# VectorE's exponential sets: the second integer addition as an accumulating transfer issued by GpSimd

## The chip, the cores and the metric
The kernel runs on one core of one Trainium2 chip. The metric is the device time of one execution in microseconds (us); lower is better. Before the change two runs took 795.1 and 797.66 us, median 796.38 us. The profile comes from a further execution of the same program, which took 790.26 us.

## The reference
The output is `g * a + (1 - g) * b`, with x of 2048 rows by 512 columns in bf16:

```python
g = sigmoid((x * gate_w).sum(-1, keepdims=True))
# a: attention with 32 heads of 16 columns
scores = einsum("bhqd,bhkd->bhqk", q, k) * 16 ** -0.5
p = softmax(scores, axis=-1)
a = einsum("bhqk,bhkd->bhqd", p, v) ... @ wo
# b: a state-space convolution, 512 channels, 128 states
P = exp(logdA[:, :, None] * l)
K = einsum("dn,dnl,dn->dl", Cc, P, dB).real
b = causal convolution of x with K (written with FFTs) + x * Dskip
```

The attention needs 32 x 2048 x 2048 exponentials. They are the largest single piece of work outside TensorE.

## The kernel before
**Tiles, quads and blocks.** A score tile holds 128 keys by 512 queries of one head. There are 2048 of them (`NSL`). Four tiles of the same 128 keys and the same 512 queries, for four heads that TensorE handles side by side, form a quad. Sixteen quads, one for each of the 16 key tiles of the sequence, form a block; 32 blocks make up the attention. All value products of a block accumulate in one bank of PSUM, `OA`. When the last quad of a block has been added, VectorE transposes `OA` out (`norm_a`), and only then can the first quad of the next block be added.

**Groups.** The scores are computed three tiles at a time. Such a group fills one of two PSUM buffers, `SC0` and `SC1`, and there are 683 groups. `qk` (line 930) issues a group's score products on TensorE. `ex` (line 945) has ScalarE take the exponential of all three tiles, or of two of them where VectorE takes the third, and writes bf16 into `ET`, a ring of 15 tiles. `pv` (line 976) multiplies a quad from `ET` with the values `VE` into `OA`.

**Sets on VectorE.** Between groups 206 and 678 VectorE takes a share of the exponentials. A set is one quad: four consecutive groups each give one tile to VectorE and two to ScalarE (`SHAPE`, line 73). `bits` (line 981) computes an affine function of the scores and stores it as 16-bit integers in the set's buffer `DZ`; read as bf16 these bits are a rough exponential. To make it less rough, three versions are added up in the value product. `batch` (line 991) issues, in this order:

1. VectorE writes `DU = DZ + 42` (line 1003, through the helper at line 996).
2. TensorE multiplies `DZ` with `VE` into `OA` (line 1008).
3. TensorE multiplies `DU` with scaled values `VS` into `OA` (line 1011).
4. VectorE adds 84 to `DZ` in place (line 1013, line 996 again).
5. TensorE multiplies the new `DZ` with the other scaled values into `OA` (line 1015), and the set is marked `dvp{i}`.

Steps 2 and 3 wait until the set's block has begun (`pv{16b}`), and from the second set on until the set before is complete (`dvp{i-1}`, line 1006).

**Which quads become sets.** `WIN` (line 78) gives two stretches of groups. From 206 to 400 only key tiles 1, 5, 9 and 13 of a block may become sets, from 400 to 678 also 3, 7 and 11 (`VKT`). Each stretch has three pairs of buffers `DZ` and `DU`, taken in turn; `clear` (line 790) refuses a new set while the set that last used its buffer is not complete. `keytile` (line 801) takes the quad from the current block while more than `LEFT` = 3 quads of it are left, and otherwise from the next block. A set is started only where the planned VectorE idle time allows (`decide`, line 831, 0.3 us of idle for each set). The last quad of a block waits in `pvq` (line 879) for the last set of the block, since it closes the accumulation.

**The order of the work.** All five instruction streams are written out ahead of time by a planner (`Sched`, lines 315 to 447). It keeps a planned clock for each engine and, group by group, issues the segments of many threads (projections, tables, convolution, normalisation, sets) where they fit. What it decides is fixed in the program: each engine runs its own stream in order and waits on semaphores for the others. For a transfer, `dma` (line 248) plans a time `c` on the issuing queue and a latency `lat` after it, and `ready` (line 182) adds a margin `DMARG` of 1.2 us before a reader is placed.

**Other work in the same time.** The convolution loads its operands by DMA on the SP queue, `WT` in 128 transfers of 256 KB and `U` in 64 of about 286 KB, and TensorE multiplies them into the bank `MB`. TensorE also issues filler products with a zero tile `wm`. GpSimd's queue holds only a few memsets and iotas.

Of the kernel before, what the change touches and what calls it, by code (L numbers as in the profile page):

```python
# [11 lines left out]
ALU = mybir.AluOpType  # L12
# [57 lines left out]
STEP = ((42, 205 / 256), (84, 166 / 256))  # L70
XB = 128 * (127 - math.log2(3.15037))
VKT = ((1, 5, 9, 13), (3, 7, 11))
SHAPE = ((2, 1),) * 4
LEFT = 3
VSW = 152
VSP = [len(k) * VSW for k in VKT]
VSAT = (200, 390)
WIN = ((206, 400, 3, 1), (400, 678, 3, 2))
DVQ = (("tabs", 0.3), (None, 1e9))
BP = 2.2  # L80
DVCAP = 2.0
BUP = 1
# [375 lines left out]
def declare(nc, es):  # L458
    B = {}

    def sb(name, free, dt=BF16):
        B[name] = Buf(name, "sb", free, dt)
# [27 lines left out]

    sb("gwT", 4)
    sb("wm", D)
    sb("x0n", 4 * D)
    sb("idf", P, FP32)
    sb("idb", P)
# [143 lines left out]
def record(nc, p, B, ins):  # L639
# [165 lines left out]
    def quad():  # L805
        if not rem:
            plan["b"] += 1
            rem.extend(ahead or block(plan["b"]))
            ahead[:] = block(plan["b"] + 1)
        q = rem.pop(0)  # L810
        pend.extend(range(4 * q, 4 * q + 4))
        if not rem:
            ends[plan["b"]] = q
        if rem or q < NQ - 16:
            todo.append((q, plan["prev"], dvps.get(plan["b"])))
        plan["prev"] = q

    def take(n, ds):
# [12 lines left out]
    def decide(g):  # L831
        while len(tiles) < min(3 * g + 3, NSL):
            x = len(tiles) // 3
            plan["used"] = max(plan["used"], idle() - DVCAP)
            if plan["set"] is None and clear(x) and idle() - plan["used"] >= dvq():
                plan["used"] += dvq()
                of, c = keytile(x)
                of.remove(c)
                w = win(x)
                r = f"{w}{sum(st['w'] == w for st in sets) % WIN[w][2]}"  # L840
                old = [i for i, st in enumerate(sets) if st["r"] == r]
                plan["set"], plan["k"], dvps[c // 16] = len(sets), 0, f"dvp{len(sets)}"
                sets.append(dict(q=c, b=c // 16, w=w, r=r, z=B["DZ" + r], u=B["DU" + r], old=old[-1] if old else None, js=[]))
            if plan["set"] is None:
                tiles.extend(take(3, []))
            else:
                st = sets[plan["set"]]
                na, nd = SHAPE[plan["k"]]
                if not pend:
                    quad()  # L850
                nxt = [pend[i % len(pend)] % 4 for i in range(na)]
                ds = sorted((j for j in range(4) if j not in st["js"]), key=lambda j: j in nxt)[:nd]
                st["js"] += ds
                got = take(na, [4 * st["q"] + j for j in ds])
                tiles.extend(got + [4 * st["q"] + j for j in ds])
                if nd:
                    vec[x] = (plan["set"], len(st["js"]) - nd, nd)
                plan["k"] += 1
                if plan["k"] == len(SHAPE):
                    plan["set"] = None  # L860
            seat()
            while todo and all(4 * todo[0][0] + j in home for j in range(4)):
                sch.add(pvq(*todo.pop(0)), 0, LAG)
# [15 lines left out]
    def pvq(q, prev, wait):  # L879
        b, kt = divmod(q, 16)  # L880
        if prev is not None:
            yield ("AFTER", f"pv{prev}")
        if ends.get(b) == q and wait:
            yield ("AFTER", wait)
        if kt == 0 and b >= 1:
            yield ("AFTER", f"n{b - 1}")
        if b < 8 and b % 2 == 0:
            yield ("AFTER", f"V{b // 2}.{kt // 4}")
        yield ("PE", QUAD)
        pv(q)  # L890
        sch.mark(f"pv{q}")
        if ends.get(b) == q:
            sch.mark(f"end{b}")
            sch.open(None)
        else:
            sch.open(b)
# [68 lines left out]
    def vscaled(k):  # L965
        kts = VKT[k]
        yield ("AFTER", f"g{VSAT[k]}")
        for pi in range(4):
            for step, (_, f) in enumerate(STEP):
                yield ("DVE", .25)  # L970
                op("DVE", lambda v, pi=pi, step=step, f=f: v.tensor_scalar(VS[k]((4 * step + pi) * VSP[k], [[VSW, len(kts)], [1, VSW]]),
                                                                           VE(pi * 4 * VG + kts[0] * VW, [[VG, len(kts)], [1, VSW]]), f, None, ALU.mult),
                   [(VE, (pi, x)) for x in range(16)], [(VS[k], (step, pi))], c=.23)
        sch.mark(f"VS{k}")
# [16 lines left out]
    def batch(i):  # L991
# [3 lines left out]
        def step(t, k, W):  # L995
            op("DVE", lambda v: v.tensor_scalar(t.u16(0, [[1, 2048]]), z.u16(0, [[1, 2048]]), float(STEP[k][0]), None, ALU.add), R, W, c=.07 + 2048 / 3840)  # L996
# [5 lines left out]
        yield ("DVE", .6, BUP)  # L1002
        step(u, 0, [(u, 0, i)])
        yield ("AFTER", f"pv{16 * b}")
        if i:
            yield ("AFTER", f"dvp{i - 1}")
        yield ("PE", QUAD)
        terms(z, None)
        yield ("AFTER", f"VS{int(q % 16 not in VKT[0])}")
        yield ("PE", QUAD)  # L1010
        terms(u, 0)
        yield ("DVE", .6, BUP)
        step(z, 1, [(z, k, (i, k, "t")) for k in range(4)])
        yield ("PE", QUAD)
        terms(z, 1)
        sch.mark(f"dvp{i}")
# [648 lines left out]
```

## Time and profile before

| | before |
|---|---|
| time of two runs, median | 796.38 us |
| time of the profiled execution | 790.26 us |
| its span | 788.5 us |
| granted TensorE clock, mean | 0.992 |
| ScalarE busy | 764.4 us (97%) |
| TensorE matmuls busy | 706.7 us (90%) |
| VectorE busy | 698.6 us (89%) |
| GpSimd busy | 11.9 us (2%) |
| moved by DMA | 76.22 MB, mean 97 GB/s |

The page counts the time in which an engine has an instruction in work; matmuls are pipelined and filler is counted with the rest. The groups of instructions give the source line, the engine, the operands (output <- inputs), the shapes, the count, the busy time, the mean duration and the idle time ahead of them with its releaser. The view by stretches cuts the span into pieces and gives in each piece the busy time and the number of instructions, the granted clock, the share of the 16 DMA engines in use and the GB/s moved.

### The profile page before, as it was taken

To read this page: it belongs to the slowest core of one execution; us is meant where nothing else is said; L and a number is where in the kernel's file an instruction comes from. 1 tells how busy PE (TensorE), PEld (TensorE's weight loads), DVE (VectorE), ACT (ScalarE), POOL (GpSimd) and SP (SyncE) were. 2 spreads that over 40 slices of the span, in tenths; PEclk is the share of its full clock that TensorE was granted. 3 is DMA by queue.
4 is the path that set the end of the run, shared out by engine and by line. 5 is a ranking of instruction groups with operands and counts; after the bars stand their busy time and mean duration, and the time that the engine had idled before them with its cause. 6 is when DMAs were issued, how large, how long until landed. Compare 5 with 4: busy or idle time off the path is not lost.

```text
span 788.5 us, 31097 instructions
## 1 busy us (share of the span) xinstructions
PE 706.7 (90%) x14262; PEld 323.0 (41%) x14262; DVE 698.6 (89%) x1078; ACT 764.4 (97%) x694; POOL 11.9 (2%) x21
## 2 busy tenths in 40 slices
PE   6778777899899989999999999999999999998996
PEld 2323322454454544434444444444444444442221
DVE  5799999999899978878797988999989999999995
ACT  5999999999999999999999999999999999999995
POOL 4000000000000000000000000000000000000000
PEclk8999999999999999999999999999999999999999
DMA  9463000000100036003665555477554556304011
GB/s 213 84 127 63 9 5 20 24 25 26 30 25 26 26 100 162 13 19 86 171 176 157 150 160 166 143 196 207 159 163 131 145 167 173 88 7 124 32 35 35
DMA packets 125923, 76.22 MB, mean 97 GB/s; under 512 B 34240, under 2 KB 116576, under 8 KB 125792
## 3 DMA queue, kind: packets, MB, share of 16 engines
q1 hardware_dynamic: 123776, 73.05, 35.1%
q8 instruction: 112, 1.84, 1.0%
q10 hardware_dynamic: 2016, 1.18, 0.7%
q14 instruction: 19, 0.16, 0.1%
HBM read 59.12 MB, written 10.63 MB: 88 GB/s over the span
## 4 chain that ended last, share of the span: by engine, by line
ACT 84%; PE 12%; DVE 2%; POOL 1%; issue 1%; ACTq 0%; POOLq 0%
ACT ET L949 84%; PE SC L655 5%; PE OA L655 4%; PE MB L655 3%; POOL VE L723 1%; DVE DZ L985 1%; DVE OT L1020 0%; DVE DZ L996 0%; DVE Ys L1331 0%; ACT fo L1627 0%; DVE sel L1305 0%; DVE KT L749 0%; DVE YJ L1353 0%; ACT ea L1098 0%; DVE OnT L1039 0%
## 5 line engine op out<-in xcount | busy, mean ns | idle before, releaser
L949 ACT ACTIVATE ET<-SC 128x1024 bf16<-128x1024 f32 (+1 forms) x683 | 756.4, 1456 | 6.3 <-PE SC L655 5.1
L655 PE MATMUL SC<-Qm,KT 32*128 32x512 bf16 x2048 | 277.9, 385 | 63.8 <-ACT ET L949 58.7
L985 DVE TENSOR_SCALAR DZ<-SC 128x512 uint16<-128x512 f32 x384 | 255.8, 684 | 41.4 <-PE SC L655 38.9
L655 PEld LDWEIGHTS SC<-Qm,KT 32*128 32x128 bf16 x2048 | 71.4, 91 | 244.7 <-ACT ET L949 209.7
L655 PE MATMUL OA<-ET,VE 128*32 128x512 bf16 x1664 | 166.0, 391 | 0.2 <-ACT ET L949 0.2
L655 PE MATMUL OA<-wm 128*32 128x512 bf16 (+3 forms) x742 | 156.8, 366 | 1.7 <-DVE wm L706 1.2
L655 PEld LDWEIGHTS MB<-U,WT 128*32 128x32 bf16 x4096 | 91.4, 153 | 32.3 <-issue 22.6
L655 PE MATMUL MB<-U,WT 128*32 128x128 bf16 (+7 forms) x4096 | 103.3, 229 | 1.5 <-issue 1.5
L655 PEld LDWEIGHTS OA<-ET,VE 128*32 128x32 bf16 x1664 | 42.5, 93 | 93.2 <-issue 91.7
L996 DVE TENSOR_SCALAR DZ<-DZ 128x2048 uint16<-128x2048 uint16 x96 | 65.6, 683 | 7.9 <-PE OA L655 7.7
L655 PE MATMUL MB<-PL,AT 128*32 128x64 bf16 (+1 forms) x2048 | 68.9, 278 | 0.1
L996 DVE TENSOR_SCALAR DU<-DZ 128x2048 uint16<-128x2048 uint16 x96 | 64.5, 685 | 0.5
L655 PEld LDWEIGHTS MB<-PL,AT 128*32 128x32 bf16 x2048 | 56.1, 139 | 11.5 <-issue 5.7
L1043 DVE TENSOR_TENSOR PL<-PL,FF 128x2048 bf16<-128x2048 bf16 x48 | 56.2, 1217 | 0.3
L655 PEld LDWEIGHTS OA<-wm 128*32 128x32 bf16 (+2 forms) x742 | 40.3, 97 | 9.1 <-issue 7.3
L655 PE MATMUL OA<-DZ,VE 128*32 128x512 bf16 x384 | 38.0, 386 | 0.0
L655 PE MATMUL OA<-DZ,VS 128*32 128x512 bf16 x384 | 37.8, 383 | 0.0
L655 PE MATMUL OA<-DU,VS 128*32 128x512 bf16 x384 | 37.7, 383 | 0.0
L1020 DVE STREAM_TRANSPOSE OT<-OA 128x512 f32<-128x512 f32 x32 | 22.7, 709 | 5.2 <-PE OA L655 5.1
L1331 DVE CAST Ys<-MB 128x512 bf16<-128x512 f32 x32 | 21.7, 679 | 0.4 <-PE MB L655 0.2
L655 PE MATMUL MB<-Wv,xT 128*32 128x128 bf16 x1024 | 19.4, 219 | 0.0
L655 PEld LDWEIGHTS MB<-Wv,xT 128*32 128x32 bf16 x1024 | 16.7, 97 | 4.0 <-issue 1.1
(133 smaller groups left out, 449.2 us busy)
## 6 DMA issues: line engine op xcount, KB each, us to landing
WT<-gm_kd SPq DMA_DIRECT2D x128, 256.0 KB, 3.5
U<-gm_xr SPq DMA_DIRECT2D x32, 288.0 KB
U<-gm_xr SPq DMA_DIRECT2D x32, 284.0 KB
gm_xr<-Xp SPq DMA_DIRECT2D x4, 576.0 KB, 5.5
gm_kd<-Ks SPq DMA_DIRECT2D x32, 64.0 KB, 1.6
gm_yn<-YJ SPq DMA_DIRECT2D x2, 1024.0 KB, 4.8
Yl<-gm_yn SPq DMA_DIRECT2D x2, 1024.0 KB, 10.6
gm_qd<-Qs SPq DMA_DIRECT2D x15, 128.0 KB, 1.7
```

Of the source, the lines that this page charges most:

```text
L655: op("PE", lambda t: t.matmul(out(), lhsT(), rhs(), start=start, stop=stop, skip_group_check=True, **kw), R, W, c=c, lat=.15, a=a, cfg=cfg)
L723: op("POOL", lambda g, pi=pi: g.memset(VE(pi * 4 * VG, [[1, 4 * VG]]), 1.0), [(idb, 0)], [(VE, (pi, k)) for k in range(16)], c=2.3)
L949: op("ACT", lambda a: a.activation(ET(512 * e, [[1, 512 * n]]), sc(0, [[1, 512 * n]]), AF.Exp, scale=DH ** -0.5), [(sc, i, g) for i in ran ...
L985: op("DVE", lambda v: v.tensor_scalar(z.u16(512 * k, [[1, 512 * n]]), sc(512 * na, [[1, 512 * n]]), XS, XB, ALU.mult, ALU.add), [(sc, na + ...
L996: op("DVE", lambda v: v.tensor_scalar(t.u16(0, [[1, 2048]]), z.u16(0, [[1, 2048]]), float(STEP[k][0]), None, ALU.add), R, W, c=.07 + 2048 ...
L1020: op("DVE", lambda v: v.transpose(OT(512 * w, [[1, 512]]), OA(0, [[1, 512]])), [(OA, 0, b)], [(OT, w, b)], c=.64)
L1043: op(eng, lambda v: v.tensor_tensor(o(), a(), b_(), f), R, W, c=c)
L1331: op("DVE", lambda v_, ys=ys: v_.tensor_copy(ys(64, [[YW, NT // 4], [1, NJ]]), MB(0, [[NJ, NT // 4], [1, NJ]])), ky, [(ys, 0, x)], c=.62)
```

## The change
Step 4 of a set is no longer an instruction of VectorE. GpSimd fills a tile `cz` of 128 x 2048 16-bit integers with 84 once, at group 200. For each set, GpSimd's queue issues a DMA from `cz` to the set's `DZ` that adds what it carries to what stands there, 4 KB for each of 128 partitions (512 KB). The planner counts 1.1 us on GpSimd's queue and 4.5 us of latency for it. Step 5 waits for it.

Around it, four more things change. A set no longer waits for the set before it (`dvp{i-1}`), so that sets' products may be added in any order; the last quad of a block therefore waits for all sets of its block, of which `dvps` now keeps a list. `LEFT` is 4. The stretch from group 270 on has four pairs of buffers; from 206 to 270 there are three as before, in a stretch of their own. The key tiles that may become sets are the same.

```diff
-LEFT = 3
+LEFT = 4
...
-WIN = ((206, 400, 3, 1), (400, 678, 3, 2))
+WIN = ((206, 270, 3, 1), (270, 400, 4, 1), (400, 678, 4, 2))
...
+    sb("cz", 2048)
...
-            todo.append((q, plan["prev"], dvps.get(plan["b"])))
+            todo.append((q, plan["prev"], tuple(dvps.get(plan["b"], ()))))
...
-                plan["set"], plan["k"], dvps[c // 16] = len(sets), 0, f"dvp{len(sets)}"
+                plan["set"], plan["k"] = len(sets), 0
+                dvps.setdefault(c // 16, []).append(f"dvp{len(sets)}")
...
-        if ends.get(b) == q and wait:
-            yield ("AFTER", wait)
+        if ends.get(b) == q:
+            for n in wait:
+                yield ("AFTER", n)
...
     def vscaled(k):
         kts = VKT[k]
         yield ("AFTER", f"g{VSAT[k]}")
+        if k == 0:
+            yield ("POOL", 2.3)
+            op("POOL", lambda g: g.memset(B["cz"].u16(0, [[1, 2048]]), STEP[1][0]), [], [(B["cz"], 0)], c=2.3)
...
         yield ("AFTER", f"pv{16 * b}")
-        if i:
-            yield ("AFTER", f"dvp{i - 1}")
         yield ("PE", QUAD)
         terms(z, None)
         yield ("AFTER", f"VS{int(q % 16 not in VKT[0])}")
         yield ("PE", QUAD)
         terms(u, 0)
-        yield ("DVE", .6, BUP)
-        step(z, 1, [(z, k, (i, k, "t")) for k in range(4)])
+        yield ("POOL", .6, BUP)
+        dma("POOL", lambda e: e.dma_start(z.u16(0, [[1, 2048]]), B["cz"].u16(0, [[1, 2048]]), accum_op=ALU.add),
+            [(B["cz"], 0)] + R, [(z, k, (i, k, "t")) for k in range(4)], c=1.1, lat=4.5)
         yield ("PE", QUAD)
         terms(z, 1)
         sch.mark(f"dvp{i}")
```

## The prediction
> **What bounds the kernel now.** I read the page's busy shares and chain first, then the groups, then the stretches of the span in which sets run.
>
> ```profile
> PE 706.7 (90%) x14262; PEld 323.0 (41%) x14262; DVE 698.6 (89%) x1078; ACT 764.4 (97%) x694; POOL 11.9 (2%) x21
> ...
> ACT 84%; PE 12%; DVE 2%; POOL 1%; issue 1%; ACTq 0%; POOLq 0%
> ...
> L949 ACT ACTIVATE ET<-SC 128x1024 bf16<-128x1024 f32 (+1 forms) x683 | 756.4, 1456 | 6.3 <-PE SC L655 5.1
> ...
> L985 DVE TENSOR_SCALAR DZ<-SC 128x512 uint16<-128x512 f32 x384 | 255.8, 684 | 41.4 <-PE SC L655 38.9
> ...
> L996 DVE TENSOR_SCALAR DZ<-DZ 128x2048 uint16<-128x2048 uint16 x96 | 65.6, 683 | 7.9 <-PE OA L655 7.7
> ...
> L996 DVE TENSOR_SCALAR DU<-DZ 128x2048 uint16<-128x2048 uint16 x96 | 64.5, 685 | 0.5
> ```
>
> ScalarE is the bound: its exponentials (L949) fill 756.4 us of a span of 788.5 us and stand idle for only 6.3 us. VectorE is not on the path; it has 96 sets (384 tiles in L985). So the 65.6 us that the addition `DZ<-DZ` takes from VectorE are worth nothing by themselves. They can only be worth something if more tiles leave ScalarE. The question is how many more sets the planner can place, and whether the new transfer makes somebody late. The next two views give, by stretch, ScalarE's exponentials and then VectorE's tiles.
>
> ```profile
> core 0: us, ACT busy (x), PEclk, DMA share, GB/s
> ...
> 50.00:250.00 200.00, 200.00 (x150) 1.00 0.14 32
> ...
> 0.00:292.00 292.00, 277.45 (x207) 0.99 0.24 52
> 292.00:492.00 200.00, 196.59 (x193) 0.99 0.46 126
> 492.00:775.00 283.00, 280.51 (x284) 1.00 0.44 124
> ```
>
> ```profile
> core 0: us, DVE busy (x), PEclk, DMA share, GB/s
> ...
> 292.00:492.00 200.00, 99.22 (x148) 0.99 0.46 126
> 492.00:775.00 283.00, 156.55 (x236) 1.00 0.44 124
> ```
>
> 207 groups have begun at 292 us and 207 + 193 = 400 at 492 us, so these two stretches are those of the code, groups 206 to 400 and 400 to 678. The first holds 148/4 = 37 sets, the second 236/4 = 59.
>
> **The worth of a set.** Without sets a group of three tiles takes 200.00/150 = 1.333 us. In the second stretch 284 - 236 = 48 groups of three take 64.0 us; the other 236 take (280.51 - 64.0)/236 = 0.917 us each. A tile moved off ScalarE saves 1.333 - 0.917 = 0.416 us, a set of four 1.66 us.
>
> **How many more sets.** A block is 64 tiles, 21.33 groups. In the first stretch only four key tiles of a block may be sets: 193/21.33 x 4 = 36.2, and 37 are there. Its key tiles are used up and the change frees none: no gain. In the second, seven may be, so the cap is one set per four groups: 278/4 = 69.5 against 59. At most 10.5 more sets, 17.5 us. Three things stand in the way of a set there now: VectorE's planned idle time, which the change relieves; a free buffer, of which there are four in place of three; and the set's own length, which grows.
>
> A set now comes every 283/59 = 4.80 us and three buffers turn over in 14.4 us. Back to back it would be 4 x 0.917 = 3.67 us. After the change a set whose block is running holds its buffer for four groups (3.67 us), the `DU` addition (0.685), two rounds of products (some 0.8, from the row of 0.39 below), the transfer as planned (0.08 + 1.1 + 4.5 + 1.2 = 6.9 us from release to reader, the code's constants) and one more round: about 12.5 us. Four buffers would allow 12.5/4 = 3.1 us, less than 3.67, so such sets don't wait. But a set taken from the next block must first wait for that block to begin, which itself waits for all sets of the block before, now slower; LEFT = 4 admits this earlier. With some 5 us more such a set holds its buffer for 17.5 us, 4.4 us per set, and as buffers go in turn it holds up the ones behind it. I take the midpoint of the present 4.80 and 3.67, rounded to the slow side: 4.3 us per set. In a stretch that shrinks to some 275 us these are 64 sets, 5 more. Gain: 5 x 1.66 = 8.3 us; bounds 0 and 17.5 us (and -3 sets, 5 us lost, if the longer hold costs more than the fourth buffer gives).
>
> **VectorE and TensorE with five more sets.** VectorE loses 96 x 0.683 = 65.6 us and gains 5 x (4 x 0.684 + 0.685) = 17 us: no bound. TensorE needs two more rounds of products per set.
>
> ```profile
> L655 PE MATMUL OA<-wm 32*128 32x512 bf16 (+2 forms) x172 | 52.6, 370 | 0.0
> ...
> L655 PE MATMUL OA<-DZ,VS 128*32 128x512 bf16 x236 | 23.2, 383 | 0.0
> ```
>
> In the stretch from 492 us one round for 59 sets takes 23.2 us, 0.39 us each; five sets add 5 x 2 x 0.39 = 3.9 us, beside 52.6 us of filler that the planner can shorten. Cost nothing; without that cover 3.9 us.
>
> **The tile of constants.** One memset of 2048 elements.
>
> ```profile
> L723 POOL MEMSET VE<- 128x2240 bf16 x4 | 7.7, 1964 | 0.3 <-DVE piota L711 0.3
> L1311 POOL MEMSET Ys<- 128x256 bf16 x4 | 1.1, 311 | 220.3 <-PE MB L655 220.3
> ```
>
> By the first row about 1.8 us, at group 200, on a queue that the second row shows idle for 220.3 us. Behind it on GpSimd are the `Ys` memsets, and the scaled values in its thread; neither is needed within those 1.8 us. Nothing.
>
> **The transfer.** The trace of before has no transfer issued by GpSimd and no adding one, so I bound its time from release to landing by its nearest rows (issues: size, median us to landing) and by how full the DMA engines are.
>
> ```profile
> q1 hardware_dynamic: 123776, 73.05, 35.1%
> ...
> WT<-gm_kd SPq DMA_DIRECT2D x128, 256.0 KB, 3.5
> ...
> gm_yn<-YJ SPq DMA_DIRECT2D x2, 1024.0 KB, 4.8
> ...
> Wo<-in_A_wo_dram SPq DMA_DIRECT2D x1, 512.0 KB, 11.5
> ```
>
> ```profile
> core 0: us, PE busy (x) PEld busy (x) DVE busy (x) ACT busy (x) POOL busy (x), PEclk, DMA share, GB/s
> ...
> 350.00:620.00 270.00, 253.59 (x5569) 122.99 (x5555) 239.13 (x394) 266.16 (x265) 0.00 (x0) 1.00 0.57 156
> 620.00:720.00 100.00, 94.36 (x1936) 43.48 (x1933) 93.90 (x154) 99.49 (x102) 0.00 (x0) 1.00 0.41 119
> 720.00:775.00 55.00, 51.00 (x634) 13.69 (x634) 52.92 (x89) 55.00 (x56) 0.00 (x0) 1.00 0.11 35
> 526.00:532.00 6.00, 4.85 (x65) 1.40 (x57) 5.42 (x10) 6.00 (x7) 0.00 (x0) 1.00 1.02 276
> ```
>
> ```profile
> L659 SPq DMA_DIRECT2D Wo<-in_A_wo_dram x1: 5517/5517/5517, 532.1 to 532.1; - x1
> ```
>
> Lower end 3.5 us (WT, half the size), upper end 11.5 us (Wo, the same size, issued at 532 us right behind the stretch with a share of 1.02). An adding transfer must read 512 KB of constants and 512 KB of `DZ`, so gm_yn, 1 MB read out of SBUF in 4.8 us, is nearest; with the planner's 1.1 us of issue 5.9 us. The reader is placed 6.9 us after the release. At 5.9 us nobody waits, and I charge 1 us in all for single late ones.
>
> Who pays when it is late: step 5 stands in TensorE's stream, and the score products of the next group are queued behind it, on which ScalarE waits. The cover is the time for which TensorE is ahead:
>
> ```profile
> PEld SC L655 <- ACT ET L949: 215.7, 457, 1.2
> ...
> DVE DZ L996 <- PE OA L655: 7.7, 14, 1.5
> ```
>
> 215.7/457 = 0.47 us per wait; what is late by more goes to ScalarE one to one. The second row (VectorE waiting for TensorE before the addition, 7.7 us) goes away and was on no path.
>
> A rule of the Trainium skill speaks against the change here: "DMA: Bandwidth & Descriptors", section "Issuing engines are not separate DMA queues", says that what GpSimd issues runs on the same 16 DMA engines as what SP issues and interleaves with it. The row of 0.57 shows those engines more than half taken; that is the second rival. Its section "SWDGE vs HWDGE vs iDMA" adds that VectorE in its two-port mode locks GpSimd out of the descriptor rings in SBUF; no run here shows that, and the only such work left in a set is the `DU` addition.
>
> **Sum.** 790.26 (profiled) - 8.3 + 1 = 783 us. The median of the runs shown is 6.1 us above the profiled execution: 789 us.
>
> **Rivals.**
> *All the sets that fit.* If the fourth buffer and the free order remove every refusal, the second stretch fills to its cap: 10.5 sets, 17.5 us, 796.4 - 17.5 = 779 us, 2.2% faster. For it: VectorE's stretch is 95% full now and gets air. Against: the longer hold of sets from the next block. Chance 0.13.
>
> *The transfer comes late: slower.* Place: 350 to 620 us, where the convolution's loads hold a share of 0.57. By q1, a full set of engines carries 73.05 MB/(0.351 x 788.5 us) = 264 GB/s; 512 KB take 2.0 us of it, 1 MB 4.0 us. With a set every 4.5 us that is a share of 0.44 to 0.89 on top of 0.57: 1.01 to 1.46, full either way. Then a transfer queues. Priced like two WT loads (2 x 3.5 us) behind 1.1 us of issue it lands after 8.1 us, 1.2 us too late; less the cover of 0.47, 0.73 us for each of some 56 sets (26 + 30 by the rates above) is 41 us: 796.4 + 41 - 8 = 829 us. It decides from (16 + 8)/56 + 0.47 + 6.9 = 7.8 us on; at Wo's 11.5 us it would cost over 200 us. Against: q1's rate is one of mostly short packets, and rows of 4 KB may be cheaper. Chance 0.31.
>
> *Nothing moves.* The longer hold eats what the fourth buffer gives: 0 to 3 sets fewer, 796 to 801 us. Chance 0.16.
>
> The forecast has the rest, 0.40, and its own range is 781 to 796 us. Two per cent, 16 us, is about what a measurement of this kernel can tell from no change. Faster by more: 0.13; within: 0.40 + 0.16 = 0.56; slower: 0.31. The range runs from 777 us, just under the first rival, to 829 us, the price of the second; above it lies about half of that rival, 0.15, below it 0.03.
>
> **What would show it.** The count of L985 in the second stretch: 236 + 20 (236 to 278). In the first: 148, give or take 4. No `DZ<-DZ` on VectorE. GpSimd's transfers with a median to landing under 6 us; over 7.8 us the second rival holds, and TensorE's waits before `OA` then name a DMA, ScalarE's idle time before L949 rises from 6.3 us, and the DMA share from 350 to 620 us nears 1. I am wrong in the sum if L985's count changes and ScalarE's total doesn't follow at 0.416 us a tile; wrong in the mechanism if the time moves with the count unchanged and no wait on a DMA.

## The result and the profile after

The change makes the kernel slower. Its median is 920.38 us (919.79 and 920.96) against 796.38 us before; the ratio is 1.156, with a 95% interval of 1.147 to 1.164. The forecast was 789 us, its range ended at 829 us. The profiled execution has a span of 919.2 us, 130.7 us more than before.

The first view is the page of the changed kernel: busy shares, DMA queues, the chain that ended last by engine and by line, the groups (line, engine, operation, tiles, count | busy us, mean ns | idle us before them and what ended it), and the transfers (size, median us to landing). L952 is before's L949, L991 its L985, L1002 its L996; L1017 is the new transfer.

```profile
PE 759.6 (83%) x14303; PEld 332.9 (36%) x14303; DVE 641.6 (70%) x972; ACT 781.1 (85%) x694; POOL 97.4 (11%) x116
...
q1 hardware_dynamic: 123776, 73.05, 31.5%
q0 software_dynamic: 13536, 49.29, 28.2%
...
ACT 38%; DMA 28%; PE 28%; DVE 2%; POOL 2%; issue 2%; ACTq 0%; POOLq 0%; DVEq 0%
ACT ET L952 38%; DMA DZ<-cz 28%; PE SC L656 11%; PE OA L656 10%; PE MB L656 7%; DVE DZ L991 1%; POOL VE L724 1%; POOL DZ L1017 1%; DVE DU L1002 0%; DVE Ys L1336 0%; DVE OT L1025 0%; ACT fo L1632 0%; DVE KT L750 0%; DVE xT L1515 0%; DVE YJ L1358 0%
...
L952 ACT ACTIVATE ET<-SC 128x1024 bf16<-128x1024 f32 (+1 forms) x683 | 773.1, 1378 | 119.7 <-PE SC L656 109.6
L991 DVE TENSOR_SCALAR DZ<-SC 128x512 uint16<-128x512 f32 x376 | 250.4, 685 | 180.4 <-PE SC L656 178.5
...
DZ<-cz POOLq DMA_DIRECT2D x94, 512.0 KB, 8.9
WT<-gm_kd SPq DMA_DIRECT2D x128, 256.0 KB, 9.3
```

ScalarE's chain of 84% has become 38%, and 28% of the chain is now "DMA", all of it waiting for the new transfer. ScalarE is idle before its exponentials for 119.7 us in place of 6.3: 113.4 us of the 130.7. Its busy time grew by 773.1 - 756.4 = 16.7 us, which is nearly all the rest; two sets fewer are 2 x 1.66 = 3.3 us of it, what the other 13.4 us are is open. VectorE has 376 tiles, 94 sets, two fewer than before. The new queue q0 takes 0.282 x 919.2 = 259 us of all 16 DMA engines, 2.76 us for each of its 94 transfers. And the convolution's loads (WT), which run beside it, land after 9.3 us in place of 3.5.

The waits of the changed kernel (who waited, for what: us in total, times, longest):

```profile
ACT ET L952 <- PE SC L656: 109.6, 107, 4.0
PEld OA L656 <- DMA DZ<-cz: 100.9, 67, 4.2
PE OA L656 <- DMA DZ<-cz: 79.2, 59, 3.9
```

TensorE's weight loads for the last round of products wait for the transfer 67 times in 94 sets, 100.9/67 = 1.5 us each. The score products of the next group are queued behind, and ScalarE waits for those. One such place in its timeline (start us, duration, engine, what; in brackets the idle time before it and its releaser):

```profile
522.44 0.40 PE L656 MATMUL OA<-DZ,VS 128*32 128x512 bf16 x4 [1.47 <-DMA DZ<-cz]
525.45 0.62 PE L656 MATMUL OA<-DZ,VS 128*32 128x512 bf16 x4 [2.01 <-DMA DZ<-cz]
526.76 0.61 PE L656 MATMUL SC<-Qm,KT 32*128 32x512 bf16 x3
527.40 1.02 ACT L952 ACTIVATE ET<-SC 128x1024 bf16<-128x1024 f32 x1 [3.17 <-PE SC L656]
```

TensorE stands 2.01 us for a transfer, then computes the scores, and the exponential begins after 3.17 us of idle time. The same matmul takes 0.40 us at 522 us and 0.62 us at 525 us. The stretches of the span show why:

```profile
core 0: us, PE busy (x) PEld busy (x) DVE busy (x) ACT busy (x) POOL busy (x), PEclk, DMA share, GB/s
...
350.00:620.00 270.00, 220.74 (x4212) 98.74 (x4209) 160.17 (x258) 210.74 (x203) 33.99 (x38) 0.84 0.83 191
620.00:720.00 100.00, 80.73 (x1720) 39.29 (x1722) 63.95 (x101) 80.78 (x79) 15.26 (x17) 0.93 0.93 210
526.00:532.00 6.00, 4.75 (x70) 1.41 (x62) 1.38 (x2) 2.05 (x2) 0.00 (x0) 0.50 0.90 222
850.00:915.00 65.00, 52.31 (x602) 14.72 (x594) 43.29 (x74) 57.43 (x57) 11.59 (x13) 1.00 0.61 123
```

The DMA share from 350 to 620 us is 0.83 (0.57 before), from 620 to 720 us 0.93 (0.41 before). TensorE's granted clock, 1.00 in both before, is 0.84 and 0.93, and 0.50 in the six microseconds behind the wait just shown. In the last stretch the convolution's loads are done; there ScalarE is busy for 57.43 us of 65 (88%) again, against 210.74 of 270 (78%) in the first. How long the transfer takes follows the same pattern (the transfer's own view, first for 550 to 650 us, then for 850 to 915 us):

```profile
L1017 POOL DMA_DIRECT2D DZ<-cz x14: 859/862/1349, 568.6 to 631.6; - x14
...
DMA to landing us min/median/max: 7.7/10.6/12.9
...
L1017 POOL DMA_DIRECT2D DZ<-cz x13: 859/859/1404, 849.9 to 902.0; - x13
...
DMA to landing us min/median/max: 4.6/6.2/8.9
```

10.6 us beside the loads, 6.2 us without them, both counted from the start of GpSimd's issue. Over the whole span 72 of the 94 transfers land after more than the 6.9 us at which their reader is planned.

### The profile page after: what moved, and what is told of

The parts are those of the page before. It is cut to its first block, busy times and chain, and to the rows that moved or that the text cites. A ratio compares the mean times of both kernels' runs of the same rounds, so it can differ in the third digit from the quotient of the medians.

```text
span 919.2 us, 31221 instructions
## 1 busy us (share of the span) xinstructions
PE 759.6 (83%) x14303; PEld 332.9 (36%) x14303; DVE 641.6 (70%) x972; ACT 781.1 (85%) x694; POOL 97.4 (11%) x116
## 4 chain that ended last, share of the span: by engine, by line
ACT 38%; DMA 28%; PE 28%; DVE 2%; POOL 2%; issue 2%; ACTq 0%; POOLq 0%; DVEq 0%
ACT ET L952 38%; DMA DZ<-cz 28%; PE SC L656 11%; PE OA L656 10%; PE MB L656 7%; DVE DZ L991 1%; POOL VE L724 1%; POOL DZ L1017 1%; DVE DU L1002 0%; DVE Ys L1336 0%; DVE OT L1025 0%; ACT fo L1632 0%; DVE KT L750 0%; DVE xT L1515 0%; DVE YJ L1358 0%
## 5 line engine op out<-in xcount | busy, mean ns | idle before, releaser
L952 ACT ACTIVATE ET<-SC 128x1024 bf16<-128x1024 f32 (+1 forms) x683 | 773.1, 1378 | 119.7 <-PE SC L656 109.6
L991 DVE TENSOR_SCALAR DZ<-SC 128x512 uint16<-128x512 f32 x376 | 250.4, 685 | 180.4 <-PE SC L656 178.5
L656 PE MATMUL SC<-Qm,KT 32*128 32x512 bf16 x2048 | 293.9, 415 | 57.9 <-ACT ET L952 53.7
L656 PE MATMUL OA<-ET,VE 128*32 128x512 bf16 x1672 | 177.4, 416 | 3.9 <-issue 3.4
L656 PE MATMUL OA<-wm 128*32 128x512 bf16 (+3 forms) x827 | 175.1, 386 | 1.2 <-DVE wm L707 1.2
L1017 POOL DMA_DIRECT2D DZ<-cz x94 | 84.0, 935 | 538.4 <-PE SC L656 327.4
L656 PE MATMUL MB<-U,WT 128*32 128x128 bf16 (+7 forms) x4096 | 111.1, 242 | 3.6 <-issue 3.4
L656 PEld LDWEIGHTS MB<-U,WT 128*32 128x32 bf16 x4096 | 96.3, 153 | 43.2 <-issue 34.7
L656 PE MATMUL OA<-DZ,VS 128*32 128x512 bf16 x376 | 45.0, 466 | 79.4 <-DMA DZ<-cz 79.2
L1002 DVE TENSOR_SCALAR DU<-DZ 128x2048 uint16<-128x2048 uint16 x94 | 63.6, 685 | 1.0
L656 PEld LDWEIGHTS OA<-wm 128*32 128x32 bf16 (+2 forms) x827 | 42.9, 99 | 12.5 <-issue 10.7
L656 PEld LDWEIGHTS OA<-DZ,VS 128*32 128x32 bf16 x376 | 10.1, 98 | 102.5 <-DMA DZ<-cz 100.9
L1336 DVE CAST Ys<-MB 128x512 bf16<-128x512 f32 x32 | 21.9, 685 | 18.2 <-PE MB L656 18.1
```

The source lines that it names most:

```text
L656: op("PE", lambda t: t.matmul(out(), lhsT(), rhs(), start=start, stop=stop, skip_group_check=True, **kw), R, W, c=c, lat=.15, a=a, cfg=cfg)
L952: op("ACT", lambda a: a.activation(ET(512 * e, [[1, 512 * n]]), sc(0, [[1, 512 * n]]), AF.Exp, scale=DH ** -0.5), [(sc, i, g) for i in ran ...
L991: op("DVE", lambda v: v.tensor_scalar(z.u16(512 * k, [[1, 512 * n]]), sc(512 * na, [[1, 512 * n]]), XS, XB, ALU.mult, ALU.add), [(sc, na + ...
L1017: dma("POOL", lambda e: e.dma_start(z.u16(0, [[1, 2048]]), B["cz"].u16(0, [[1, 2048]]), accum_op=ALU.add), [(B["cz"], 0)] + R, [(z, k, (i, ...
L1336: op("DVE", lambda v_, ys=ys: v_.tensor_copy(ys(64, [[YW, NT // 4], [1, NJ]]), MB(0, [[NJ, NT // 4], [1, NJ]])), ky, [(ys, 0, x)], c=.62)
```

## The experiments

The theory from these views: the transfer takes too much of the 16 DMA engines, so it lands after its planned place, and TensorE's stream stops for it. Its rivals were that the loss comes from the fourth buffer, the free order or `LEFT`; that it is only the sharing with the convolution's loads; that GpSimd's path is slow whatever the size; and that the transfer harms others by its load alone, without anybody waiting for it. Each expectation names the theories that were open when it was written. All edits are to the changed kernel. Ratios are to the kernel before on the same chip, whose medians there were 788.7 to 790.0 us.

### Everything but the transfer

The addition goes back to VectorE, with the rest of the change kept:

```diff
-        yield ("POOL", .6, BUP)
-        dma("POOL", lambda e: e.dma_start(..., accum_op=ALU.add), ..., c=1.1, lat=4.5)
+        yield ("DVE", .6, BUP)
+        step(z, 1, [(z, k, (i, k, "t")) for k in range(4)])
```

> The second addition goes back to VectorE; the windows, the four buffers, LEFT = 4 and the free order of the sets stay as in the changed kernel. If the transfer is the whole loss, no wait on it is left and the time is within 2% of the kernel before, 782 to 812 us, with about 96 sets and a clock near 0.99. If the rest of the change is to blame (order, LEFT, the list of sets that a block's end waits for), it stays above 880 us. In between, both have a part.

Measured: 806.81 us, ratio 1.023 (1.017 to 1.029), 96 sets. The same with `LEFT = 3`, as before the change:

```diff
-LEFT = 4
+LEFT = 3
```

> The run with the addition on VectorE (806.8 us, 2.3% above the kernel before), now with LEFT = 3 as before; what then remains of the change is the free order of the sets, the fourth buffer and the list at a block's end. If LEFT = 4, which takes sets from the next block earlier, makes those 18 us, this kernel is within 1% of the kernel before, about 789 us. If the free order or the list does, it stays at 800 us or more.

Measured: 789.27 us, ratio 0.998 (0.995 to 1.001), 96 sets. The exponentials' rows, the first kernel's and then the second's:

```profile
L952 ACT ACTIVATE ET<-SC 128x1024 bf16<-128x1024 f32 (+1 forms) x683 | 759.1, 1423 | 17.1 <-PE SC L656 16.1
```

```profile
L952 ACT ACTIVATE ET<-SC 128x1024 bf16<-128x1024 f32 (+1 forms) x683 | 755.5, 1455 | 7.1 <-PE SC L656 6.8
```

So the fourth buffer, the free order and the tile of constants cost nothing and bring nothing: 96 sets, as before. Between these two only `LEFT` differs, 1.023 against 0.998; further down it is seen not to be a cost of `LEFT` as such. Then the whole change, transfer included, with `LEFT = 3`:

> The whole change with LEFT = 3 in place of 4 and nothing else. On VectorE the same step gave 789.3 in place of 806.8 us. If LEFT's part is additive, this kernel is 15 to 20 us under the changed one, 1.13 to 1.14 times before. If LEFT = 4 is needed because the sets at a block's end are complete later with the transfer, it is no faster, 1.15 times before or more.

Measured: 913.58 us, ratio 1.160 (1.156 to 1.164), 96 sets. Between this kernel and the one above only the transfer differs: 0.998 against 1.160. The transfer, with the places that the planner gives it and its reader, accounts for the whole loss. What `LEFT = 3` gave with VectorE's addition it does not give here.

### What a further set is worth

Here the second addition is left out altogether, with no transfer; the last round reads its tile as it was:

```diff
-        yield ("POOL", .6, BUP)
-        dma("POOL", lambda e: e.dma_start(..., accum_op=ALU.add), ..., c=1.1, lat=4.5)
```

> The second addition is left out altogether (the third round of products reads DZ without the 84 added), with no transfer; windows, buffers, LEFT and order as in the changed kernel. It shows what the change could give at best if the addition cost nothing and nobody waited. By the prediction's sum each set more is worth 1.66 us: with about 104 sets, 8 more than before, 783 us. If sets beyond those of before are worth nothing, because something other than the number of tiles on ScalarE decides, 795 us or more.

Measured: 805.76 us, ratio 1.021 (1.016 to 1.025), with 104 sets. The row of the exponentials on its page and a line of its waits (`fo` is the last step of the output, which takes the output projection from the bank `MB`):

```profile
L952 ACT ACTIVATE ET<-SC 128x1024 bf16<-128x1024 f32 (+1 forms) x683 | 743.5, 1383 | 7.6 <-PE SC L656 6.9
```

```profile
ACT fo L1629 <- PE MB L656: 31.0, 1, 31.0
```

Eight more sets take 756.4 - 743.5 = 12.9 us off ScalarE, as the prediction had it (8 x 1.66 = 13.3). But the convolution now ends late (its last product begins at 749 us, before at 707), and ScalarE waits 31.0 us at the end for the output projection, which comes behind it. The next kernel gives the convolution an earlier place in the plan:

```diff
-OVER = 0.3
+OVER = 0.45
-CUP = (2.0, .9)
+CUP = (2.0, .3)
```

> The run without the addition (104 sets, 805.8 us, ScalarE waiting 31.0 us at its end for the output projection) with two of the planner's constants moved so that the convolution's products are placed ahead of other filler work (CUP's second value 0.3 in place of 0.9, OVER 0.45 in place of 0.3); the addition stays left out. If more sets brought nothing because the convolution and the output projection behind it then end last, that wait falls below 10 us and the time to 770 to 785 us, under the kernel before. If sets beyond those of before are worth nothing for another reason, it stays at 795 us or more.

Measured: 793.76 us, ratio 1.005 (1.002 to 1.009), with 103 sets. ScalarE is busy for 745.2 us, but idle before its exponentials for 18.2. Both kernels still had `LEFT = 4`, which could have taken the gain. So both again with `LEFT = 3`, first with the earlier convolution:

```diff
-LEFT = 4
+LEFT = 3
```

> Left out: the second addition of every set (the last round of products reads the tile as it was). The convolution's earlier place in the plan is kept, LEFT goes back to 3. If a set is worth 1.66 us of the span, and LEFT = 4 alone hid that in the kernel with the same constants (1.005, exponentials idle 18.2 us), the 2% that LEFT = 4 cost with VectorE's addition come back: some 7 more sets than 96 give 7 x 1.66 = 11.6 us, ratio 0.98 to 0.99, ScalarE idle before its exponentials under 10 us. If TensorE does not feed ScalarE faster whatever LEFT is, the ratio stays at 0.995 to 1.01 and the idle time above 15 us.

Measured: 787.81 us, ratio 0.999 (0.995 to 1.003), with 103 sets. Its exponentials, and a line of its waits:

```profile
L952 ACT ACTIVATE ET<-SC 128x1024 bf16<-128x1024 f32 (+1 forms) x683 | 745.4, 1388 | 10.8 <-PE SC L656 9.7
```

```profile
ACT fo L1629 <- PE MB L656: 10.3, 1, 10.3
```

ScalarE is busy for 756.4 - 745.4 = 11.0 us less than before (7 x 1.66 = 11.6 were to be had). Of these 10.8 - 6.3 = 4.5 us come back as waits for scores, and 10.3 - 4.6 = 5.7 us as a longer wait for the output projection at the end (4.6 us is that wait's row in the kernel before), although the convolution's last product begins at 701 us here. Together 10.2. The second addition cost nothing here, neither on VectorE nor by a transfer, and the time is that of before: what further sets take off ScalarE, TensorE does not follow in this order. The ratio lies in the second theory's range, the idle time between the two: the gain is gone as the second said, but half of it in another place. The other one:

> Left out: the second addition of every set. LEFT = 3, the convolution's place as in the changed kernel. If the late convolution is what takes back the gain of more sets, ScalarE again waits about 30 us at the end for the output projection and the ratio is 1.01 to 1.02. If LEFT = 4 was at fault there, that wait falls under 10 us and the ratio to 0.985 to 1.0.

Measured: 814.52 us, ratio 1.034 (1.029 to 1.039), with 103 sets. Its waits:

```profile
ACT fo L1629 <- PE MB L656: 38.0, 1, 38.0
```

The profiled execution took 822.55 us, the three others 813.4 to 814.7. With the convolution late again (its last product begins at 757 us), the wait takes the gain back with `LEFT = 3` too, by more than either theory had it, and here `LEFT = 3` is the slower one (1.034 against 1.021). So `LEFT` has no sign of its own: every edit of the plan shifts the whole order, and the kernels with neither a transfer nor GpSimd's addition lie between 0.998 and 1.034.

### The load without a reader

To part the late reader from the load, the transfer adds into two scratch tiles that nobody reads, from the 17th set on; the addition itself is left out as above:

```diff
+        if i >= 17:
+            yield ("POOL", .6, BUP)
+            zs = B[f"zs{i % 2}"]
+            dma("POOL", lambda e: e.dma_start(zs.u16(0, [[1, 2048]]), B["cz"].u16(0, [[1, 2048]]), accum_op=ALU.add),
+                [(B["cz"], 0)] + R, [(zs, 0)], c=1.1, lat=4.5)
```

> As the run without the addition, but GpSimd still issues the adding transfer for each set from the 17th on, 512 KB into one of two scratch tiles that nobody reads. The load on the DMA engines is there and the reader's wait is not. If the loss comes from TensorE waiting for the transfer, the time is within 15 us of the run without the addition. If it comes from the convolution's loads, which landed after 9.3 us in place of 3.5 in the changed kernel, it is above 850 us and TensorE's waits name WT or U.

Measured: 881.54 us, ratio 1.118 (1.112 to 1.124). The row of the exponentials (L954 here), then lines of its waits:

```profile
L954 ACT ACTIVATE ET<-SC 128x1024 bf16<-128x1024 f32 (+1 forms) x683 | 747.2, 1360 | 63.4 <-PE SC L658 61.8
```

```profile
PEld SC L658 <- DMA Qm<-gm_qd: 40.1, 8, 19.7
ACT fo L1640 <- PE MB L658: 45.1, 1, 45.1
...
SPq L1299 <- DMA U<-gm_xr: 131.2, 48, 5.2
```

TensorE never waits for the transfer, and yet 1.118 - 1.021 = 9.7% are lost against the kernel without it. TensorE waits eight times for the small `Qm` loads (queries), up to 19.7 us. They stand in SP's queue, and that queue waits 131.2 us at L1299, where the convolution's loads are issued, for earlier such loads (33.8 us in the kernel without the transfer). The longest of the eight waits ended at 593.7 us, and the loads that it waited for were issued from 588.5 us on: they were late in the queue, not on the way. The convolution ends late (its last product begins at 809 us), and ScalarE waits 45.1 us for the output projection, 14.1 us more than without the transfer. That the transfer does its harm only through its reader is refuted.

The same with a plain copy in place of the addition:

```diff
-            dma("POOL", lambda e: e.dma_start(zs..., B["cz"]..., accum_op=ALU.add),
+            dma("POOL", lambda e: e.dma_start(zs..., B["cz"]...),
```

> The run with the unread transfer (881.5 us, software queue 27.5% of the engines for 87 transfers, 2.77 us each), with a plain copy of the same 512 KB in place of the adding one. If adding costs the engines about twice a copy because each byte of the destination is read as well, the queue's share halves to about 14% (1.4 us each) and the time lies between 806 and 881 us, near 840. If adding is no dearer than copying, share and time stay.

Measured: 816.70 us, ratio 1.033 (1.027 to 1.039). The queue's row (packets, MB, share of the 16 engines over the span):

```profile
q0 software_dynamic: 12528, 45.62, 16.3%
```

0.163 x 813.1/87 = 1.52 us of all engines for each copy of 512 KB. The adding transfers of the changed kernel take 2.76 us, 1.8 times as much, and the copy costs 1.2% where the unread additions cost 9.7%, at the same places in the same order. So it is mostly the adding that fills the engines. The Trainium skill, "Collectives: The Full Stack", section "The bandwidth ceiling: the fold count and why AG ≠ RS ≠ AR", says of another operation, ReduceScatter, that its addition by DMA needs two source reads and so runs at about half the rate of AllGather's copy. The 1.8 measured here is near that; that the second read is the reason here too, no run shows.

### A later reader

The planner is told 8.0 us in place of 4.5, so it puts the reader later:

```diff
-            ..., c=1.1, lat=4.5)
+            ..., c=1.1, lat=8.0)
```

> The changed kernel with the transfer's latency planned at 8.0 us in place of 4.5, so that its reader is placed 10.4 us after the release in place of 6.9; the transfer itself is the same. Buffers are held longer and the planner finds room for 87 sets in place of 94. If the loss comes from the reader being placed too early, TensorE's waits on the transfer (100.9 and 79.2 us in the changed kernel) fall below 30 us each and the time falls below 850 us. If the load on the DMA engines is the larger part, by what it does to the convolution's loads and the queue of SP, the time stays above 870 us although those waits are gone.

Measured: 897.07 us, ratio 1.133 (1.125 to 1.141), 87 sets.

```profile
L952 ACT ACTIVATE ET<-SC 128x1024 bf16<-128x1024 f32 (+1 forms) x683 | 778.9, 1429 | 89.9 <-PE SC L656 81.3
```

```profile
PEld OA L656 <- DMA DZ<-cz: 13.6, 11, 2.7
...
PE MB L656 <- DMA U<-gm_xr: 38.9, 9, 7.9
```

The wait for the transfer fell from 100.9 to 13.6 us, but the ratio only from 1.156 to 1.133; seven sets fewer are 7 x 1.66 = 11.6 us against it. The convolution's own products now wait for their loads (U, 38.9 us). The changed kernel has no such wait; that its wait for the transfer had covered this one is argued.

### Lighter loads beside it

The convolution's loads are cut to a quarter of their bytes from the fourth of each kind on; its result is then not computed from whole data:

```diff
-   ... [[NT * 16 * PC, nb], [1, NT * 16]] ...
+   ... [[NT * 16 * PC, nb if v < NWT else nb // 4], [1, NT * 16]] ...
-   ... [[1, n]] ...
+   ... [[1, n if x < NU else n // 4]] ...
```

> The changed kernel with the convolution's loads cut to a quarter of their bytes after the first three of each kind (the rest of the operands is stale, so the convolution's result is left wrong); all instructions and waits stay. If the transfer is late because it shares the DMA engines with these loads, it lands after about 6 us as it does in the changed kernel after 850 us (median 6.1), ScalarE's idle time falls below 40 us, and the time is 790 to 820 us. If the transfer by itself is too slow, landing stays near 8.9 us and the time above 880 us.

Measured: 874.09 us, ratio 1.107 (1.103 to 1.111).

```profile
q1 hardware_dynamic: 79232, 37.51, 17.6%
q0 software_dynamic: 13536, 49.29, 29.8%
...
L952 ACT ACTIVATE ET<-SC 128x1024 bf16<-128x1024 f32 (+1 forms) x683 | 770.8, 1384 | 77.2 <-PE SC L656 69.9
...
DZ<-cz POOLq DMA_DIRECT2D x94, 512.0 KB, 7.1
```

About a third of the loss goes with half of q1's bytes: 1.156 became 1.107, between the two theories. The transfer still takes 0.298 x 874.4/94 = 2.77 us of the engines and lands after 7.1 us; 50 of the 94 land after more than the 6.9 us of their readers, and TensorE's weight loads still wait 63.0 us for them. The load without a reader costs 9.7%, the reader beside light loads 10.7%, both together 16%: this suggests that they hide each other in part. With both taken away, the reader planned later and the loads light:

```diff
-            ..., c=1.1, lat=4.5)
+            ..., c=1.1, lat=8.0)
-   ... [[NT * 16 * PC, nb], [1, NT * 16]] ...
+   ... [[NT * 16 * PC, nb if v < NWT else nb // 4], [1, NT * 16]] ...
-   ... [[1, n]] ...
+   ... [[1, n if x < NU else n // 4]] ...
```

> The whole transfer, its reader planned 8.0 us behind the issue in place of 4.5, and the convolution's loads cut to a quarter from the fourth of each kind on (its result is then not computed from whole data). If the late reader and the late loads are two causes that hide each other, this kernel has neither: TensorE's waits for the transfer under 15 us and for U and WT under 10 us, ratio 1.02 to 1.05, clock above 0.97. If the transfer does harm in a third way that neither edit touches (its load on the other users of SBUF or on SP's queue), the ratio stays above 1.08.

Measured: 845.37 us, ratio 1.071 (1.066 to 1.076), 87 sets. The exponentials, a line of the waits, and two lines of the timeline:

```profile
L952 ACT ACTIVATE ET<-SC 128x1024 bf16<-128x1024 f32 (+1 forms) x683 | 775.3, 1441 | 40.4 <-PE SC L656 33.4
```

```profile
PEld OA L656 <- DMA DZ<-cz: 1.4, 2, 1.0
```

```profile
305.34 0.61 PE L656 MATMUL SC<-Qm,KT 32*128 32x512 bf16 x3
...
308.40 2.37 ACT L952 ACTIVATE ET<-SC 128x1536 bf16<-128x1536 f32 x2 [2.63 <-PE OA L656]
```

The waits for the transfer are gone (1.4 us), and no wait for `U` or WT of the convolution shows, yet 7% remain, between the two theories (2 to 3% of it could be the order, which is another one). Of the 54.5 us by which its span is longer than before's, 18.9 us are ScalarE's busy time (9 fewer sets are 9 x 1.66 = 15 us of it) and 34.1 us its idle time, for which no load is named. The two lines show a place where it is the clock: TensorE is busy throughout there, but its granted clock is 0.50 from 304 to 313 us, a round of scores takes 0.61 us in place of 0.39, and ScalarE waits 2.63 us. This place is not the transfer's doing: the single-column products of the gate (128x1) run there, and the clock is at 0.50 from 305 to 308 us in the kernel before and from 305 to 314 us in the one with VectorE's addition and `LEFT = 4`. It shows what a lower clock costs; how often it is low has to be counted.

The count is read from the stretches view, cut into slices of 1 us from 100 us on. In the kernel before, 4 slices of 688 have a granted clock of 0.55 or less. In the changed kernel they are 145 of 819, in 21 spells of 2 to 13 us; ScalarE is busy for 56% of these 145 and for 92% of the 639 slices at 0.95 or more. 145 x 0.44 = 64 us of its idle time lie at half clock, 639 x 0.08 = 51 us at full clock. So the clock is a third part; whether each of these spells costs the idle time in it, or the same late transfer makes both, a count cannot tell. In the kernel with both causes taken away 48 of 743 slices are at half clock, with 48 x 0.36 = 17 us of the 51 us that ScalarE is idle from 100 us on; for the rest of that idle time no cause is shown. With `LEFT = 4` and VectorE's addition it is 30 of 706 slices, with `LEFT = 3` and VectorE's addition 9 of 689. In these the count rises with the ratio, but not strictly over all kernels: the one at 1.034 has 61 of 720.

### Fewer bytes

The transfer adds a quarter of the columns, then half of them; the rest of the tile stays without its second addition:

```diff
-   z.u16(0, [[1, 2048]]), B["cz"].u16(0, [[1, 2048]])
+   z.u16(0, [[1, 512]]), B["cz"].u16(0, [[1, 512]])
```

> The changed kernel with the transfer adding to only 512 of the 2048 columns, 128 KB in place of 512 KB (three of a set's four tiles lack the addition); order, waits and planned latency stay. If the bytes on the DMA engines are the cause, the software queue's share falls from 28.2% to about 7%, the transfer lands in about 4 us, inside the 6.9 us, and the time is that of the run with the addition on VectorE, 800 to 820 us. If a fixed delay of GpSimd's path is the cause, landing stays above 6 us and the time above 860 us.

Measured: 802.87 us, ratio 1.018 (1.009 to 1.026). The page of this kernel:

```profile
q0 software_dynamic: 13536, 12.33, 10.3%
...
L952 ACT ACTIVATE ET<-SC 128x1024 bf16<-128x1024 f32 (+1 forms) x683 | 760.9, 1437 | 13.0 <-PE SC L656 7.0
...
DZ<-cz POOLq DMA_DIRECT2D x94, 128.0 KB, 4.1
```

> The changed kernel with the transfer adding to 1024 of the 2048 columns, 256 KB (two of a set's four tiles lack the addition). From the full transfer (2.76 us of all 16 engines) and the quarter (0.88 us) this one should hold them for 1.5 us. If the loss grows evenly with the bytes, the time lies midway on the line from the quarter (802.9 us) to the whole (1.1557 times before, about 912 us): 839 us. If it only begins where landing passes the 6.9 us at which the reader is placed, landing has a median near 6 us and the time is 805 to 820 us.

Measured: 828.84 us, ratio 1.050 (1.044 to 1.056). The page of the half:

```profile
q0 software_dynamic: 13536, 24.65, 17.5%
...
DZ<-cz POOLq DMA_DIRECT2D x94, 256.0 KB, 5.7
```

All three sizes have the same number of issues on the same queue, the same plan and 94 sets. Issue and path on GpSimd cost nothing that shows: the quarter (1.018) is no slower than the kernel with VectorE's addition and `LEFT = 4` (1.023). Engine time goes 0.88, 1.54, 2.76 us a transfer, landing 4.1, 5.7, 8.9 us, the ratio 1.018, 1.050, 1.156. A loss even in the bytes would put the half at 1.018 + 0.138/3 = 1.064 (839 us, as expected above); measured is 1.050 (1.044 to 1.056), between that and the other theory's 805 to 820 us. So the loss rises somewhat faster than the bytes, without a sharp edge at 6.9 us. The parts rise with it: 8, 30 and 72 of 94 transfers land after more than 6.9 us, TensorE's weight loads wait 2.9, 26.9 and 100.9 us for them, and 16 of 700, 42 of 727 and 145 of 819 slices are at half clock.

### The addition on GpSimd itself

With the plan's constants of the second kernel without the addition, GpSimd adds in place of a transfer (planned 2.2 us):

```diff
-        dma("POOL", lambda e: e.dma_start(..., accum_op=ALU.add), ..., c=1.1, lat=4.5)
+        op("POOL", lambda g: g.tensor_scalar(z..., z..., float(STEP[1][0]), None, ALU.add), R, ..., c=2.2)
```

> As the run before it, with the addition back and done by GpSimd itself, one instruction on DZ of 128 x 2048 16-bit integers, planned at 2.2 us, and no transfer. If only the bytes on the DMA engines made GpSimd the wrong place for it, the time is 770 to 790 us, at or under the kernel before, with WT landing after some 4 us as before. If GpSimd's instruction takes much more than the 2.2 us planned (its memset of the same size takes 1.8 us), or slows VectorE's additions beside it, TensorE waits for GpSimd before the third round and the time is above 800 us.

Measured: 1135.19 us, ratio 1.435 (1.428 to 1.442). The row of the addition, and the view of `DU` (duration min/median/max in ns):

```profile
L1017 POOL TENSOR_SCALAR DZ<-DZ 128x2048 uint16<-128x2048 uint16 x101 | 555.4, 5509 | 286.2 <-PE OA L656 228.6
```

```profile
L1002 DVE TENSOR_SCALAR DU<-DZ x101: 643/1771/5853, 296.9 to 1111.2; 128x2048 uint16<-128x2048 uint16 x101
```

The addition takes 5.5 us on GpSimd (VectorE: 0.683). VectorE is not the reason: the one of the 101 that ran with no instruction of VectorE beside it took 5.358 us. VectorE's own addition goes from 0.685 to 1.771 us in the median, to 5.9 at worst: 65 of its 101 ran beside one of GpSimd's and took 3.9 us in the median, the other 36 took 0.683. No kernel of these runs is clearly faster than the kernel before; the nearest that computes the same, with the addition on VectorE and `LEFT = 3`, takes the same time.

## Why the prediction was wrong

**What bounds the kernel** was read too simply. ScalarE at 97% is the bound of the kernel as it stands, and taking tiles off it does shorten its busy time at 1.66 us a set, as worked out: 12.9 us for eight sets, 11.0 us for seven. The step that failed is the one from there to the span. The kernels without the addition returned all of it, or more, as waits for TensorE, at the scores or at the end. The prediction had the two further rounds of products of each set "cost nothing" because the planner could shorten the filler. It did not: the zero-tile products into `OA` went from 742 (156.8 us) to 774 with 104 sets and to 803 (162.2 us) with 103. That this is what held the scores back is argued.

**How many more sets** failed. 64 were forecast in the second stretch. These are the changed kernel's tiles on VectorE by stretch; group 400 falls at 550 us:

```profile
core 0: us, DVE busy (x), PEclk, DMA share, GB/s
...
290.00:550.00 260.00, 96.35 (x144) 0.84 0.76 173
550.00:903.00 353.00, 154.08 (x232) 0.89 0.83 184
```

144/4 = 36 and 232/4 = 58, against 37 and 59 before: the first count is as forecast; the second is one set fewer than before, below the forecast of 64 and its bound of no gain, and inside the three sets fewer that stand in brackets there. The fourth buffer does not make up for the longer hold; with a still longer one (8.0 us) there are 87, and with no second addition 104.

**VectorE, GpSimd's queue and the tile of constants** were right: VectorE has 30% of its time free, and the kernel with all of this but the transfer and `LEFT = 4` runs at 0.998.

**The transfer** is the step that decided. "At 5.9 us nobody waits", charged with 1 us in all, took the row of gm_yn, 1 MB read out of SBUF in 4.8 us, as nearest, and added 1.1 us of issue that the row, counted from the issue's start, already holds. The transfer landed after 8.9 us, and TensorE's weight loads waited 100.9 us for it; even without other loads the median was 6.2 us, and 4.6 was the best of all. A plain write is no measure for an adding transfer: the copy of the same size holds the engines for 1.52 us, the adding one for 2.76. The upper end of 11.5 us held for the median, not for each transfer: one of the 14 in the view above took 12.9 us.

**The second rival** was the right mechanism in each of its signs: a DMA named in TensorE's waits before `OA`, ScalarE's idle time up, the share at 0.83 and 0.93. Its engine time of 2.0 to 4.0 us a transfer holds the measured 2.76. Its price, 41 us, was a third of the loss. It put the landing at 8.1 us and the harm at 0.73 us for 56 sets; measured are 1.5 us in each of 67 waits, and two further parts that it had not: the loads that get late in their turn, on which SP's queue and the convolution depend, and TensorE's clock, at half for 145 us in place of 4. With a share of 1.01 to 1.46 worked out in the prediction itself, the landing should not have been priced like two loads from a half-empty system, and this case should have had more than 0.31.

The rule of the Trainium skill that was set against the change there ("DMA: Bandwidth & Descriptors", section "Issuing engines are not separate DMA queues") is borne out by WT's landing, 3.5 us before and 9.3 us after. Its other one, that VectorE in its two-port mode locks GpSimd out of the descriptor rings, shows at most faintly. In the kernel with the unread addition an issue with no `DU` addition beside it took 0.88 us at most, one with it 0.08 us more in the mean and up to 1.35 us; in the one with the copy it is 0.53 us at most, 0.09 us more and up to 1.02 us. It did not make the transfers late: in the changed kernel the 30 issues beside a `DU` addition landed after 8.4 us in the median, the other 64 after 9.3.

What stays open is how the three parts (the late reader, the late loads, the clock) divide the loss. They were not held apart: no run kept the clock up while TensorE waited. That TensorE's waits bring the clock down is argued, from 0.50 right behind waits in the changed kernel; the place at 304 us shows that it also falls where TensorE does not wait. Why orders without a transfer differ by 2 to 3% is open too; the slower ones have more slices at half clock, or an output projection that ends later.

## What to carry to other kernels

Before work moves from an engine to DMA, sum the DMA engines' time, not the bytes: an addition in SBUF counted 1.8 copies here, and where the sum of the shares reaches 1, price a queue, with everybody who loads through the same engines, and not a duration. Relieving an engine that is 97% busy brought nothing here, because its supplier did not go faster; a kernel that leaves the moved work out altogether shows what there is to win (here 0.999 in the best of four orders: nothing). A latency that is planned by hand should be checked at the load under which it will run: 6.2 us in an empty stretch were 10.6 us in a full one.

## What the runs showed of the hardware

- An adding transfer of 512 KB in SBUF, issued by GpSimd, took 2.76 us of all 16 DMA engines (256 KB: 1.54, 128 KB: 0.88; a copy of 512 KB: 1.52).
- GpSimd's addition on 128 x 2048 uint16 took 5.5 us in the mean and 5.36 us with VectorE idle, a memset of that size 1.8 us. VectorE's addition took 3.9 us in the median beside it, up to 5.9 us, and 0.683 us otherwise. The Trainium skill, "GPSIMD Engine Reference", section "Engine selection", calls operations with one input on GpSimd roughly line rate; measured here, the distance to VectorE is eightfold.
- TensorE's granted clock fell to 0.50 within microseconds of waits of 1.5 and 2.0 us and stayed there for about ten, though TensorE was busy again; the same matmul took 0.62 us in place of 0.40. Over the whole span it was 0.906, before 0.992. About half of ScalarE's idle time from 100 us on (64 of 129 us) lies in such spells. Between single-column products the clock also fell to 0.50, at 304 to 306 us, in kernels with and without a transfer, while the profile shows TensorE busy.
